# Second-layer tile stores and loads cut by groups of 32 partitions, spaced 7 units apart, with weights asked for 12 units ahead

## The chip, the cores and the metric

The kernel runs on one core of a Trainium2 chip. The time is the device time of one execution in microseconds; the median of three runs of the kernel before is 1767.69 us (1763.55, 1767.69 and 1768.19).

## The reference

```python
def _moe2_ref(x, U, V, w_ch1, w_ch2):
    xt = x.transpose(0, 2, 1)
    h = xt @ U @ V
    u = x + h.transpose(0, 2, 1)
    ch = np.maximum(u @ w_ch1, 0.0) @ w_ch2
    return (u + ch).astype(np.float32)

def reference(**kwargs):
    ...
    attn_out = _attn_ref(**attn_kwargs)
    B, H, S, D = attn_out.shape
    x = np.ascontiguousarray(attn_out.transpose(0, 2, 1, 3)).reshape(B, S, H * D)
    x = _moe_ref(x=x, **moe_kwargs)
    return _moe2_ref(x=x, **moe2_kwargs)
```

q, k and v are float32 of (8, 8, 576, 64). Attention works within chunks of 64 rows. Both layers that follow work on 8*576 = 4608 rows of 512 columns with weights of 512x2048 and 2048x512, which come in as float64. The first layer normalises its rows; the second adds a product of rank 32 along the sequence (U and V) before its two matrix products.

## The kernel before

The 4608 rows are 36 tiles of 128 rows. The first layer runs over 12 blocks of 3 tiles together with the attention, and leaves each finished tile in DRAM (`x1_d`, `store`, L698). It ends at about 965 us of the span. The second layer, which the change concerns, takes the rows in five passes `s` of 6, 8, 8, 8 and 6 tiles (`SB`). One pass is 2*7*8 = 112 units (`UNITS`): 7 products of 8 units for the first weight matrix and 7 products of 8 units for the second (a Strassen scheme with 7 block products). A unit is six matmuls of 128x128 against 512 columns (384 in the first and the last pass), and needs one weight tile of 128x512 float32, 256 KB.

**Weights.** `w_in(n)` (L973) issues the DMA of the weight tile of unit `n` from DRAM on the queue of SP (SyncE). 15 buffers are used in turn (`NWR`), so the tile of unit `n` can only be written when the matmuls of unit `n - 15` are over. At unit `n` the program issues `w_in(n + 14)` and then the side tasks of the unit.

**Side tasks.** A table (`side(u, fn, args)`) hangs further work on units. Each engine and each DMA queue takes its instructions strictly in program order; an instruction that waits holds up those behind it. For each of the tiles of the next pass:

- `x1_load` (L790) loads a tile of the first layer's result from DRAM into a window `xw` (two buffers) with four DMAs of 64 KB on SP's queue. Each of the four takes a block of 32 rows and spreads it over all 128 partitions, 512 bytes per run.
- `x1_turn` (L796) transposes the window into the operand `u` on DVE (VectorE), 11 units later.
- `low` (L808) adds the rank-32 product on top: matmuls into `pslow`, and an add on DVE (L823).

For each tile of the pass before:

- `y_turn` (L957) transposes the finished tile on DVE into `zt` (two buffers in turn).
- `y_store` (L965) stores `zt` to the output three units later, with four DMAs of 64 KB on SP's queue, again one for each block of 32 rows, from all 128 partitions. In the last pass half of them go on ScalarE's queue. A later `y_turn` into the same buffer waits until these DMAs have landed.

For each of the eight batches `z_load` (L647) loads the rank-32 sums with DMAs of 256 KB, each of which writes the same 32 rows to four groups of partitions (`to_broadcast([4, 32, DM])`), `z_sum` adds on GpSimd (L654) and `z_rep` copies on ScalarE (L661) and subtracts on DVE (L662). The first and the third pass hold two batches each, the second and the fourth one each, the last none.

On DVE the same queue also holds what PE (TensorE) needs: the evacuation of each product from PSUM (`g1_evac` L903, `g2_evac` L926) and the low parts of the operands (`h_lo` L882). So a `y_turn` or `x1_turn` that waits for a DMA holds up PE.

Of the kernel before, what the change touches and what calls it, by code (L numbers as in the profile page):

```python
# [18 lines left out]
def fused_kernel(ctx, tc, q, k, v, g_ln, w1_a, w2_a, U, V, w1_b, w2_b, out):  # L19
    nc = tc.nc  # L20
# [4 lines left out]
    P = 128  # L25
# [7 lines left out]
    SB = (6, 8, 8, 8, 6)  # L33
# [667 lines left out]

    O = (0, 1, 5, 6, 4, 2, 3)
    W_AT = ((0, 2, 6, 1, 3, 4, 5), (6, 0, 5, 1, 2, 3, 4))
    UNITS = 2 * 7 * NPR
    ORDER = []
    for a, b in ((0, 1), (2, 2), (3, 3), (4, 5), (6, 6)):
# [9 lines left out]
    def unit(n):  # L716
# [3 lines left out]
            return (s, which) + ORDER[r]  # L720
        return s, which, stages(s)[r // NPR], r % NPR
    NWR, NHR = 15, 8
    row0 = [sum(SB[:s]) * P for s in range(len(SB))]
    ncol = [SB[s] * P // 2 for s in range(len(SB))]
    made = {}
# [64 lines left out]
    def x1_load(s, t):  # L790
        i = row0[s] // P + t
        w = win[s, t] = t1.tile([P, 4, P], F32, tag=("w", "cvd")[i % 2], name="xw")
        for a in range(4):
            nc.sync.dma_start(out=w[:, a], in_=x1_d[i][32 * a:32 * a + 32].rearrange("j (g c) -> g j c", g=4))  # L794

    def x1_turn(s, t):  # L796
        w = win.pop((s, t)).rearrange("p a (i k) -> p a k i", k=KT)
# [167 lines left out]
    def y_store(s, t):  # L965
        z_tile(s, t)
        r = row0[s] + t * P
        z = zout.pop((s, t)).rearrange("p (a c) -> p a c", a=4)
        for a in range(4):
            eng = nc.scalar if s == len(SB) - 1 and a % 2 else nc.sync  # L970
            eng.dma_start(out=out[r:r + P].rearrange("(a j) (g c) -> a g j c", a=4, g=4)[a], in_=z[:, a])  # L971

    def w_in(n):  # L973
        if n < len(SB) * UNITS:
            s, which, i, p = unit(n)
            nc.sync.dma_start(out=f32(wring(n)), in_=w_d[which, p][W_AT[which][O[i]]])  # L976

    tasks = {}

    def side(u, fn, a):  # L980
        tasks.setdefault(u, []).append((fn, a))
# [4 lines left out]
    def all_units():  # L986
        late = []
        ps1, banks2 = {}, {}
        nb = 0
        for n in range(len(SB) * UNITS):  # L990
            s, which, i, p = unit(n)
            N = ncol[s]
            last = n >= len(SB) * UNITS - NPR
            chain = i in (1, 5)
            w_in(n + NWR - 1)
            for fn, a in tasks.pop(n, ()):
                fn(*a)
            if which == 0:
                if not chain:
                    tags = G1B if n < 20 else G1B + G2B[2:]  # L1000
                    ps1[p] = psp.tile([P, DM], F32, tag=tags[nb % len(tags)], name="ps1")
                    nb += 1
                ps = ps1[p]
                hi, lo = xring(s, i)
                w = w_of(n)
                c = 0
                for k_ in range(2):
                    for l, x in ((w(0, k_), hi), (w(0, k_), lo), (w(1, k_), hi)):
                        mm(ps[:, :N], l, x[:, k_], start=c == 0 and not chain, stop=c == 5, skip_group_check=i in (0, 1, 4, 5))
                        c += 1  # L1010
                late.append((g1_evac, (s, i, p, ps)))
            else:
                if p == 0 and not chain:
                    banks2[i] = [psp.tile([P, DM], F32, tag=G2B[2 * (i in (2, 4)) + t], name="ps2") for t in range(2)]
                ps2 = banks2[i - chain]
                for t in range(2):
                    todo = [p]
                    if last:
                        todo = range(NPR) if p == NPR - 1 else ()
                    for pp in todo:  # L1020
                        hi, lo = (a[:, :N] for a in hring((7 * s + stages(s).index(i)) * NPR + pp))
                        w = w_of(n - p + pp)
                        for c, (l, x) in enumerate(((w(0, t), hi), (w(0, t), lo), (w(1, t), hi))):
                            mm(ps2[t][:, :N], l, x, start=pp == 0 and c == 0 and not chain, stop=pp == NPR - 1 and c == 2, skip_group_check=i in (0, 1, 4, 5))
                    if p == NPR - 1 and not last:
                        g2_evac(s, i, (t,), ps2)
                    if last and todo:
                        g2_evac(s, i, (t,), ps2)
                        for tt_ in range(SB[s] // 2):
                            y_turn(s, tt_, (2 + t, 3 + t))  # L1030
                            if t:
                                y_store(s, tt_)
            while len(late) > (which == 0):
                fn, a = late.pop(0)
                fn(*a)
            yield n
# [3 lines left out]
    def l2_first(at):  # L1040
        e = NF * (NB - 1)
        for b in range(2):
            g = e - 1 + 6 * b
            at(g, z_load, b, 0)
            at(g, z_load, b, 1)
            for m in (1, 2, 3):
                at(g + 1 + m, z_sum, b, m)
                if m < 3:
                    at(g + 1 + m, z_load, b, m + 1)
            at(g + 5, z_rep, b)  # L1050
        for t in range(SB[0]):
            at(e + (0, 2, 2, 4, 5, 6, 7)[t], x1_load, 0, t)
            at(e + (2, 4, 5, 6, 7, 8, 9)[t], x1_turn, 0, t)
        for n, part in enumerate(low_parts(0)):
            at(e + 9 + n // 2, low, 0, part, ("m0", "m1"))
        for n in range(NWR - 1):
            at(e + 6 + n // 2, w_in, n)
        at(e + 12, x_hi, 0, 0)
        for k_ in range(2):
            at(e + 12, x_lo, 0, 0, k_, nc.vector)  # L1060
        x_parts(1, 0, 1, nc.vector)
        x_parts(4, 0, 2, nc.vector)
        done = 1
        for s in range(len(SB)):
            u0 = s * UNITS
            for i, u in ((3, 14), (4, 19), (5, 26), (6, 31)):
                x_parts(u0 + u, s, i, nc.gpsimd)
            for p in range(NPR):
                h_parts(u0 + 38 + p, s, 0, p)
                side(u0 + (43 if p < 4 else 47) + p % 4, h_t1, (s, p))  # L1070
                side(u0 + 51 + p, h_t, (s, 3, p))
                for i in range(1, 7):
                    h_parts(u0 + 56 + 8 * stages(s).index(i) + p - 7, s, i, p)
            if s:
                for t in range(2):
                    side(u0 + 1 + t, u_adds, (s - 1, t))
                for t in range(SB[s - 1]):
                    side(u0 + 8 + 5 * t, y_turn, (s - 1, t))
                    side(u0 + 11 + 5 * t, y_store, (s - 1, t))
            if s + 1 < len(SB):  # L1080
                turned = []
                for t in range(SB[s + 1]):
                    u = u0 + 14 + 6 * t
                    side(u, x1_load, (s + 1, t))
                    side(u + 11, x1_turn, (s + 1, t))
                    turned.append(u + 11)
                z0 = u0
                ready = 0
                for part in low_parts(s + 1):
                    b = part[2]  # L1090
                    if b > done:
                        for g in range(2):
                            side(z0, z_load, (b, g))
                        for g in (1, 2, 3):
                            z0 += 6
                            side(z0, z_sum, (b, g))
                            if g < 3:
                                side(z0, z_load, (b, g + 1))
                        z0 = ready = max(ready + 1, z0 + 2)
                        side(z0, z_rep, (b,))  # L1100
                        ready += 2
                        z0 += 1
                        done = b
                    ready = max(ready, turned[part[3]]) + 1
                    side(ready, low, (s + 1, part, G2B[:2] if ready < u0 + 54 else G1B))
                assert ready < u0 + 82, ready - u0
                x_parts(u0 + 96, s + 1, 0, nc.vector, 2)
                x_parts(u0 + 100, s + 1, 1, nc.vector, 2)
                x_parts(u0 + 105, s + 1, 2, nc.vector, 2)
            else:  # L1110
                for t in range(2):
                    side(u0 + 56 + 34 + 6 * t, u_adds, (s, t))
                n = SB[s] // 2
                for t in range(n):
                    side(u0 + 105 + t, y_turn, (s, n + t))
                    side(u0 + 107 + t, y_store, (s, n + t))
                    side(u0 + 108 + t, y_turn, (s, t, (0, 2)))


    with tc.manual_schedule():  # L1120
# [23 lines left out]
        for n in range(2, NB):  # L1144
            g = NF * (n - 1)
# [260 lines left out]
```

## Time and profile before

| what | value |
| --- | --- |
| median of three runs | 1767.69 us |
| the profiled execution | 1765.53 us |
| its span | 1763.7 us |
| PE busy (pipelined matmuls) | 1647.9 us, 93% |
| DVE, ScalarE, GpSimd busy | 1208.5, 599.4, 303.6 us |
| HBM read, written | 241.53 MB, 64.49 MB |

The span is one execution as the hardware profiler saw it; 1.8 us lie around it. PE's busy time counts overlapping matmuls, so that its share alone does not tell how close it is to its limit; the idle time and the time of one unit do. "DMA share" is the mean busy share of the core's 16 DMA engines.

### The profile page before, as it was taken

How to read it: one execution, taken by the hardware profiler on the slowest of the kernel's cores; microseconds unless marked ns; L12 is line 12 of the kernel's file. 1: busy time of each engine (PE TensorE's matmuls, PEld its weight loads, DVE VectorE, ACT ScalarE, POOL GpSimd, SP SyncE). 2: the span in 40 equal slices, each digit the busy share in tenths (PEclk: the TensorE clock that was granted, in tenths of full speed). 3: DMA queues.
4: the chain of work that ended last, by engine and by line, in shares of the span. 5: the costliest groups of instructions: out<-in, count | busy, mean ns of one | idle time of the engine just before them, and what ended most of it. 6: DMA issues, size and time to landing. Idle time of an engine off the chain costs nothing.

```text
span 1763.7 us, 27789 instructions
## 1 busy us (share of the span) xinstructions
PE 1647.9 (93%) x9902; PEld 1429.2 (81%) x9902; DVE 1208.5 (69%) x2226; ACT 599.4 (34%) x1098; POOL 303.6 (17%) x291
## 2 busy tenths in 40 slices
PE   6899999999999999999998889989995999899996
PEld 5788887888888888888887889868874888678995
DVE  7888645687777888788743368379535963785585
ACT  5554311223333332232321244334423343344342
POOL 1000001202111111111210240430133005301311
PEclk8899999999999999999999989999997999999998
DMA  6443333556557566575533678667765766677783
GB/s 168 114 138 108 84 83 87 148 146 167 166 143 200 161 170 177 151 213 157 180 112 117 199 222 282 195 218 247 194 191 168 226 193 192 204 231 198 244 275 114
DMA packets 380492, 307.90 MB, mean 175 GB/s; under 512 B 189505, under 2 KB 276545, under 8 KB 380354
## 3 DMA queue, kind: packets, MB, share of 16 engines
q1 hardware_dynamic: 317490, 247.12, 49.2%
q10 hardware_dynamic: 62864, 59.00, 10.5%
q8 instruction: 80, 1.31, 0.3%
q14 instruction: 58, 0.48, 0.1%
HBM read 241.53 MB, written 64.49 MB: 174 GB/s over the span
## 4 chain that ended last, share of the span: by engine, by line
PE 59%; DMA 7%; DVE 5%; SPq 2%; issue 1%; ACT 1%; POOL 0%; DVEq 0%; POOLq 0%; ACTq 0%
PE ps L66 32%; PE acc L66 13%; PE psh L66 12%; DMA zr<-zd 2%; DMA out<-zt 2%; DMA wr<-wd 1%; PE psm L66 1%; DMA xw<-x1d 1%; SPq L794 1%; DVE zt L963 1%; PE zps L66 1%; PE pslow L66 1%; SPq L971 0%; SPq L976 0%; POOL zr L654 0%
## 5 line engine op out<-in xcount | busy, mean ns | idle before, releaser
L66 PE MATMUL ps<-act,wr 128*128 128x512 f32 (+1 forms) x2100 | 460.3, 376 | 36.9 <-DVE h L918 9.8
L66 PEld LDWEIGHTS ps<-act,wr 128*128 128x128 f32 x2100 | 390.0, 192 | 96.2 <-issue 20.7
L66 PE MATMUL psh<-act,w0h 128*128 128x384 f32 x1536 | 398.4, 340 | 7.4 <-DVE act L679 2.8
L66 PE MATMUL acc<-w1h,act 128*128 128x512 f32 x1152 | 400.1, 401 | 1.6 <-DVE xbig L696 1.6
L66 PEld LDWEIGHTS psh<-act,w0h 128*128 128x128 f32 x1536 | 285.1, 190 | 26.7 <-DVE act L679 3.8
L66 PEld LDWEIGHTS acc<-w1h,act 128*128 128x128 f32 x1152 | 217.2, 189 | 58.7 <-issue 7.9
L66 PE MATMUL psh<-act,w0l 128*128 128x384 f32 x768 | 261.3, 340 | 0.9 <-DVE w0l L158 0.9
L679 DVE SCALAR_TENSOR_TENSOR act<-psh,act 128x384 fp32r<-128x384 f32 x192 | 106.8, 556 | 186.4 <-ACT act L678 185.9
L66 PE MATMUL acc<-w1l,act 128*128 128x512 f32 x576 | 228.1, 396 | 0.0
L678 ACT ACTIVATE act<-psh 128x384 fp32r<-128x384 f32 x192 | 94.0, 489 | 347.3 <-PE psh L66 284.2
L66 PEld LDWEIGHTS psh<-act,w0l 128*128 128x128 f32 x768 | 146.1, 190 | 1.2 <-DVE w0l L158 1.2
L66 PEld LDWEIGHTS acc<-w1l,act 128*128 128x128 f32 x576 | 108.7, 189 | 17.6
L908 ACT ACTIVATE h<-h 128x512 f32<-128x512 f32 (+1 forms) x80 | 45.8, 588 | 159.9 <-DVE h L918 120.0
L618 POOL TENSOR_TENSOR act<-wT,act 128x512 fp32r<-128x512 f32 x27 | 34.9, 1294 | 303.1 <-ACT act L617 303.1
L544 POOL TENSOR_SCALAR rs<-mv 128x1 f32<-128x1 f32 x36 | 10.9, 302 | 402.2 <-DVE mv L542 393.9
L914 DVE TENSOR_TENSOR h<-ps,h 128x512 f32<-128x512 f32 (+1 forms) x40 | 23.8, 628 | 62.9 <-PE ps L66 47.6
L654 POOL TENSOR_TENSOR zr<-zr 128x512 f32<-128x512 f32 x24 | 31.1, 1297 | 201.2 <-DMA zr<-zd 190.1
L197 ACT ACTIVATE raw<-raw 128x512 f32<-128x512 f32 x64 | 42.7, 675 | 53.1 <-DVE raw L228 13.4
L901 POOL TENSOR_TENSOR h<-h,h 128x512 f32<-128x512 f32 (+1 forms) x40 | 49.1, 1242 | 45.4 <-ACT h L908 25.0
L963 DVE STREAM_TRANSPOSE zt<-xbig 128x512 f32<-128x512 f32 (+1 forms) x16 | 15.3, 974 | 53.7 <-DMA out<-zt 36.0
L963 DVE STREAM_TRANSPOSE zt<-qk 128x256 f32<-128x256 f32 (+2 forms) x26 | 16.8, 690 | 45.0 <-DMA out<-zt 26.5
L564 POOL TENSOR_TENSOR xn<-xn,gbc 128x512 f32<-128x512 f32 x27 | 38.6, 1430 | 50.5 <-DVE xn L563 50.5
(218 smaller groups left out, 2623.5 us busy)
## 6 DMA issues: line engine op xcount, KB each, us to landing
wr<-wd SPq DMA_DIRECT2D x560, 256.0 KB
raw<-in_moe_w_ch SPq DMA_DIRECT2D x48, 512.0 KB
w<-sp ACTq DMA_DIRECT2D x54, 256.0 KB
wd<-wsp ACTq DMA_DIRECT2D x38, 256.0 KB
xw<-x1d SPq DMA_DIRECT2D x144, 64.0 KB
x1d<-xbig SPq DMA_DIRECT2D x34, 256.0 KB
v_pl<-in_v SPq DMA_DIRECT2D x132, 64.0 KB
out<-zt SPq DMA_DIRECT2D x132, 64.0 KB
```

What stands on the lines that cost most here:

```text
L66: nc.tensor.matmul(o, lhsT=l, rhs=r, start=start, stop=stop, **kw)
L197: nc.scalar.activation(out=w.bitcast(F32), in_=w.bitcast((F32, U32)[n]), func=AF.Copy, scale=2.0 ** (-112, -52)[n])
L564: nc.gpsimd.tensor_tensor(out=xn, in0=xn, in1=gbc, op=ALU.mult)
L618: nc.gpsimd.tensor_tensor(out=lo, in0=x, in1=f32(hi), op=ALU.subtract)
L654: nc.gpsimd.tensor_tensor(out=zr[:, 0], in0=zr[:, 0], in1=zr[:, 1], op=ALU.add)
L678: nc.scalar.activation(out=hi, in_=ps, func=AF.Relu)
L679: nc.vector.scalar_tensor_tensor(out=lo, in0=ps, scalar=0.0, in1=f32(hi), op0=ALU.max, op1=ALU.subtract)
L794: nc.sync.dma_start(out=w[:, a], in_=x1_d[i][32 * a:32 * a + 32].rearrange("j (g c) -> g j c", g=4))
L901: nc.gpsimd.tensor_tensor(out=b11, in0=b12, in1=b11, op=ALU.subtract)
L908: relu = lambda a: nc.scalar.activation(out=a, in_=a, func=AF.Relu)
L914: vt(out=c12, in0=ps, in1=c12, op=ALU.add)
L963: nc.vector.transpose(out=z[:, :, a:b], in_=u[:, a - k0:b - k0, o].rearrange("p k (a j) -> p a k j", j=32))
```

## The change

The four DMAs of `x1_load` and of `y_store` are cut in another way: each now moves one group of 32 partitions, with four runs of 512 bytes for each partition, where it moved one block of 32 rows to or from all 128 partitions. Bytes, number of DMAs and length of a run stay. `y_turn` of tile `t` stands at unit 8 + 7t of the pass (8 + 5t before) and `y_store` three units later as before; `x1_load` stands at unit 10 + 7t (14 + 6t) and `x1_turn` 11 units later as before. At unit `n` the program now issues `w_in(n + 12)`; there are still 15 buffers.

```diff
+    YT, XT = (8, 7, 3), (10, 7, 11)
...
     NWR, NHR = 15, 8
+    WL = NWR - 3
...
-        for a in range(4):
-            nc.sync.dma_start(out=w[:, a], in_=x1_d[i][32 * a:32 * a + 32].rearrange("j (g c) -> g j c", g=4))
+        for g in range(4):
+            nc.sync.dma_start(out=w[32 * g:32 * g + 32], in_=x1_d[i][:, g * P:(g + 1) * P].rearrange("(a j) c -> j a c", j=32))
...
-        for a in range(4):
-            eng = nc.scalar if s == len(SB) - 1 and a % 2 else nc.sync
-            eng.dma_start(out=out[r:r + P].rearrange("(a j) (g c) -> a g j c", a=4, g=4)[a], in_=z[:, a])
+        for g in range(4):
+            eng = nc.scalar if s == len(SB) - 1 and g % 2 else nc.sync
+            eng.dma_start(out=out[r:r + P, g * P:(g + 1) * P].rearrange("(a j) c -> j a c", j=32), in_=z[32 * g:32 * g + 32])
...
-            w_in(n + NWR - 1)
+            w_in(n + WL)
...
-                    side(u0 + 8 + 5 * t, y_turn, (s - 1, t))
-                    side(u0 + 11 + 5 * t, y_store, (s - 1, t))
+                    side(u0 + YT[0] + YT[1] * t, y_turn, (s - 1, t))
+                    side(u0 + YT[0] + YT[1] * t + YT[2], y_store, (s - 1, t))
...
-                    u = u0 + 14 + 6 * t
+                    u = u0 + XT[0] + XT[1] * t
                     side(u, x1_load, (s + 1, t))
-                    side(u + 11, x1_turn, (s + 1, t))
+                    side(u + XT[2], x1_turn, (s + 1, t))
```

SP's queue in the third pass, before: from the load of tile 112 to that of tile 113 (`xw` is the load's window, `zt` a store's source, `wr` a weight buffer; the last part of a row is the shape that the DMA writes).

```order
L794 DMA xw<-x1d_112 128x1x128 x4
L976 DMA wr_9357<-wd_5_131 128x512
L976 DMA wr_9450<-wd_6_132 128x512
L971 DMA out<-zt 4x32x128 x4
L976 DMA wr_9140<-wd_7_133 128x512
L976 DMA wr_9142<-wd_0_126 128x512
L976 DMA wr_9172<-wd_1_127 128x512
L976 DMA wr_9174<-wd_2_128 128x512
L794 DMA xw<-x1d_113 128x1x128 x4
```

The same stretch of SP's queue now:

```order
L796 DMA xw<-x1d_112 32x4x128 x4
L978 DMA wr_9244<-wd_7_133 128x512
L973 DMA out<-zt 32x4x128 x4
L978 DMA wr_9279<-wd_0_126 128x512
L650 DMA zr<-zd_147 128x1x512
L978 DMA wr_9281<-wd_1_127 128x512
L978 DMA wr_9317<-wd_2_128 128x512
L978 DMA wr_9319<-wd_3_129 128x512
L978 DMA wr_9446<-wd_4_130 128x512
L978 DMA wr_9458<-wd_5_131 128x512
L796 DMA xw<-x1d_113 32x4x128 x4
```

A store led by 4 becomes one led by 32, and so does the source of a load; seven weight tiles lie between two loads instead of six, and a store follows its load after one of them.

DVE's queue at the start of the third pass, before (L914 and L916 are evacuations that PE waits for, L963 is `y_turn`, L801 `x1_turn`):

```order
L963 STREAM_TRANSPOSE zt<-xbig 128x4x4x32
L914 TENSOR_TENSOR h_0_9604<-ps_12224,h_0_9604 128x512
L914 TENSOR_TENSOR h_0_9618<-ps_12235,h_0_9618 128x512
L801 STREAM_TRANSPOSE xbig<-xw 128x4x4x32
L916 TENSOR_TENSOR h_2_9674<-ps_12244,h_0_9472 128x512
L916 TENSOR_TENSOR h_2_9689<-ps_12254,h_0_9483 128x512
L916 TENSOR_TENSOR h_2_9702<-ps_12274,h_0_9503 128x512
L963 STREAM_TRANSPOSE zt<-xbig 128x4x3x32
```

The same stretch now:

```order
L965 STREAM_TRANSPOSE zt<-xbig 128x4x4x32
L916 TENSOR_TENSOR h_0_9597<-ps_12208,h_0_9597 128x512
L916 TENSOR_TENSOR h_0_9607<-ps_12219,h_0_9607 128x512
L916 TENSOR_TENSOR h_0_9621<-ps_12228,h_0_9621 128x512
L918 TENSOR_TENSOR h_2_9677<-ps_12242,h_0_9469 128x512
L918 TENSOR_TENSOR h_2_9692<-ps_12255,h_0_9481 128x512
L918 TENSOR_TENSOR h_2_9705<-ps_12266,h_0_9501 128x512
L803 STREAM_TRANSPOSE xbig<-xw 128x4x4x32
L918 TENSOR_TENSOR h_2_9719<-ps_12278,h_0_9512 128x512
L965 STREAM_TRANSPOSE zt<-xbig 128x4x4x32
```

Line numbers are two higher in the changed file. Between two `y_turn`s stand seven evacuations instead of five. The work itself is the same on every engine.

## Rows read from the trace of the kernel before

**Rows 1.** The page, parts 1 (busy time) and 4 (the chain, shares by line).
```profile
PE 1647.9 (93%) x9902; PEld 1429.2 (81%) x9902; DVE 1208.5 (69%) x2226; ACT 599.4 (34%) x1098; POOL 303.6 (17%) x291
...
PE ps L66 32%; PE acc L66 13%; PE psh L66 12%; DMA zr<-zd 2%; DMA out<-zt 2%; DMA wr<-wd 1%; PE psm L66 1%; DMA xw<-x1d 1%; SPq L794 1%; DVE zt L963 1%; PE zps L66 1%; PE pslow L66 1%; SPq L971 0%; SPq L976 0%; POOL zr L654 0%
```

**Rows 2.** Busy time in stretches: the five passes, then the tail.
```profile
core 0: us, PE busy (x) PEld busy (x) DVE busy (x) ACT busy (x) POOL busy (x), PEclk, DMA share, GB/s
967.00:1111.00 144.00, 130.94 (x707) 124.99 (x706) 92.10 (x170) 54.12 (x109) 28.84 (x26) 0.96 0.75 234
1111.00:1273.00 162.00, 156.16 (x683) 127.38 (x682) 110.16 (x173) 62.78 (x105) 35.52 (x30) 1.00 0.70 212
1273.00:1457.00 184.00, 162.84 (x694) 132.65 (x693) 111.63 (x177) 63.66 (x106) 41.55 (x33) 0.94 0.66 194
1457.00:1623.00 166.00, 157.81 (x687) 127.97 (x685) 108.00 (x172) 62.29 (x105) 38.33 (x29) 0.99 0.68 206
1623.00:1747.00 124.00, 119.90 (x673) 117.79 (x672) 81.98 (x150) 47.90 (x98) 35.51 (x32) 0.99 0.72 230
1747.00:1764.00 17.00, 0.00 (x0) 0.00 (x0) 4.84 (x13) 0.00 (x0) 0.00 (x0) 0.58 0.24 71
```

**Rows 3.** Timeline of ScalarE: first and 16th evacuation of the second and last pass.
```profile
1112.34 0.59 ACT L910 COPY h<-ps 128x512 f32<-128x512 f32 x1 [4.83 <-PE ps L66]
...
1132.73 0.60 ACT L912 ACTIVATE h<-ps 128x512 f32<-128x512 f32 x1 [0.76 <-PE ps L66]
...
1624.64 0.48 ACT L910 COPY h<-ps 128x384 f32<-128x384 f32 x1 [7.12 <-PE ps L66]
...
1640.24 0.49 ACT L912 ACTIVATE h<-ps 128x384 f32<-128x384 f32 x1 [0.55 <-PE ps L66]
```

**Rows 4.** Waits from 960 us on: total us, times, longest us.
```profile
DVE zt L963 <- DMA out<-zt: 62.5, 19, 8.1
...
DVE xbig L801 <- DMA xw<-x1d: 15.0, 4, 8.5
```

**Rows 5.** Timeline of DVE in the third pass: two `y_turn`s, idle before in brackets.
```profile
1332.08 0.85 DVE L963 STREAM_TRANSPOSE zt<-xbig 128x384 f32<-128x384 f32 x1 [8.07 <-DMA out<-zt]
...
1345.18 0.85 DVE L963 STREAM_TRANSPOSE zt<-xbig 128x384 f32<-128x384 f32 x1 [7.76 <-DMA out<-zt]
```

**Rows 6.** Timeline of SP's queue in the third pass: a held-up store and a free one.
```profile
1319.61 7.33 SPq L971 DMA_DIRECT2D out<-zt  x4
...
1360.41 2.43 SPq L971 DMA_DIRECT2D out<-zt  x4
```

**Rows 7.** Stretch of the tail with only stores: length, PE, clock, DMA share, GB/s.
```profile
1758.00:1759.00 1.00, 0.00 (x0) 0.50 0.29 87
```

**Rows 8.** SP's timeline and a stretch (columns as in 7): weight loads by 32 partitions.
```profile
57.25 1.74 SPq L130 DMA_DIRECT2D raw<-in_moe_w_ch  x4
...
59.00:60.00 1.00, 0.53 (x2) 0.50 0.91 268
```

**Rows 9.** Issues on SP's queue by line: duration ns min/median/max, first and last start.
```profile
L130 SPq DMA_DIRECT2D raw<-in_moe_w_ch x64: 311/428/1624, 5.0 to 176.6; - x64
...
L976 SPq DMA_DIRECT2D wr<-wd x560: 314/325/2145, 922.7 to 1731.1; - x187
...
L971 SPq DMA_DIRECT2D out<-zt x132: 536/567/2496, 1126.8 to 1755.8; - x132
```

**Rows 10.** Timeline of GpSimd in the first pass: a `z_sum` and what it waited for.
```profile
1013.93 1.27 POOL L654 TENSOR_TENSOR zr<-zr 128x512 f32<-128x512 f32 x1 [14.38 <-DMA zr<-zd]
```

**Rows 11.** Busy time in a stretch at the end of the first layer.
```profile
940.00:960.00 20.00, 16.59 (x79) 14.97 (x80) 7.06 (x12) 3.77 (x7) 1.85 (x2) 0.83 0.29 109
```

**Rows 12.** Timelines of SP's queue and of DVE in the tail.
```profile
1740.97 15.32 SPq L971 DMA_DIRECT2D out<-zt  x12
...
1746.93 0.63 DVE L963 STREAM_TRANSPOSE zt<-qk 128x256 f32<-128x256 f32 x1 [4.60 <-DMA out<-zt]
```

**Rows 13.** Busy time in a stretch in the middle of the second pass.
```profile
1202.00:1212.00 10.00, 10.00 (x45) 7.88 (x44) 10.00 (x19) 5.40 (x9) 0.00 (x0) 1.00 0.85 298
```

More of the change, by code (lines that the diff above doesn't have):

```diff
@@ L1055, in l2_first @@
             at(e + 9 + n // 2, low, 0, part, ("m0", "m1"))
-        for n in range(NWR - 1):
+        for n in range(WL):
             at(e + 6 + n // 2, w_in, n)
@@ L1082, in l2_first @@
                 for t in range(SB[s + 1]):
-                    u = u0 + 14 + 6 * t
+                    u = u0 + XT[0] + XT[1] * t
                     side(u, x1_load, (s + 1, t))
-                    side(u + 11, x1_turn, (s + 1, t))
-                    turned.append(u + 11)
+                    side(u + XT[2], x1_turn, (s + 1, t))
+                    turned.append(u + XT[2])
                 z0 = u0
```

## The prediction

> **What bounds the kernel now.** I read the page first, then stretches of the second layer, then what ended the waits there. PE is busy for 93% of the span, and its matmuls make up most of the chain; of DMAs the chain names the z loads, the stores of `zt` and the window loads with 1 to 2% each [rows 1]. So a gain can only come from stretches in which PE stands still or runs at the low clock, and these have to be sized.
>
> For that I need the length of a unit at full rate. In the second pass 15 units take 1132.73 - 1112.34 = 20.39 us, so 1.36 us; in the last pass 1640.24 - 1624.64 = 15.6 us, so 1.04 us [rows 3]. A pass of 112 units should take 152.2 or 116.5 us. The stretches of [rows 2] are cut one unit before each pass's first evacuation. From the 512-column passes I take off 2 us for the `pslow` matmuls (an estimate), and from the first pass 8 us for first-layer matmuls still among its units, `pslow` and `zps`. What is lost:
>
> - first pass: 144 - 116.5 - 8 = 19.5 us
> - second: 162 - 154.2 = 7.8 us
> - third: 184 - 154.2 = 29.8 us, at a mean clock of 0.94
> - fourth: 166 - 154.2 = 11.8 us
> - last: 124 - 116.5 = 7.5 us
> - tail, with PE idle: 17 us
>
> Together 93 us. Inside the passes DVE waits 62.5 us for output stores to land, in 19 places, and 15 us for window loads [rows 4]; in the third pass two `y_turn`s stand 8.07 and 7.76 us each [rows 5], with PE's evacuations queued behind them. Stores are late at their issue too: four took 7.33 us on SP's queue, where four others took 2.43 us [rows 6], and the weights queue behind.
>
> **Why the transfers are slow.** In the tail, with nothing but stores under way, the DMA share is 0.29 and 87 GB/s move [rows 7], though 24 DMAs are queued. That is little more than 4 of 16 engines, and the shape of a store is led by 4. I read it so: a store, a window load (its source is led by 4) and a z load (4 copies in front) each use four engines only, the same four, at 87/4 = 21.8 GB/s each. Against that, four weight loads by groups of 32 partitions, issued in 1.74 us, move 268 GB/s at a share of 0.91 [rows 8]. The new DMAs are led by 32 as well.
>
> [...]
>
> **A bound per pass.** I count what the four engines must move in the first 60 units of a pass, where the side tasks lie. A weight tile puts 16 KB on each, a tile's load or store 64 KB before and 16 KB now, a z load 64 KB in both. At 21.8 GB/s:
>
> - third pass (8 loads, 8 stores, 8 z loads): 0.98 + 0.52 + 0.52 + 0.52 = 2.55 MB, 117 us, where 60 units last 82 us: 35 us over. Now 0.98 + 0.13 + 0.13 + 0.52 = 1.77 MB, 81 us: just level.
> - second (4 z loads): 23 us over before, now 69 of 82 us.
> - fourth (6 loads, 4 z loads): 17 us over, now below 69 us.
> - last (stores alone): 69 of 62 us, 7 over; now 51.
> - first (8 loads, 8 z loads): 93 of 62 us, 31 over; now 75, still 13 over.
>
> The order of these overruns (35, 31, 23, 17, 7) is near that of the losses (29.8, 19.5, 7.8, 11.8, 7.5); 15 weight buffers absorb a part.
>
> **The change part by part.**
>
> - Third pass: 24 of 29.8 us go. The z loads stay on four engines, which come out just level, so some 5 us of waits remain. Bounds 12 and 29.
> - Second pass 7 of 7.8 us (bounds 3 and 7.8), fourth 10 of 11.8 us (6 and 11.8): the overrun is gone.
> - Last pass: 5 of 7.5 us (1 and 7).
> - First pass: 13 of 31 us of overrun stays, so 19.5 x 13/31 = 8 us of loss; 11 us go. What holds up the rest is a z sum, which stands 14.38 us before its DMA lands [rows 10]. Bounds 0 and 16.
> - End of the first layer, where window and z loads for the first pass share the four engines: PE is busy 16.59 of 20 us in one stretch, at a clock of 0.83 and a DMA share of 0.29 [rows 11]. The window loads get out of the z loads' way: 3 us (0 and 6).
> - Tail: `y_turn` waits 4.60 us for a store, and SP needs 15.32 us to issue 12 stores, as the engines are full [rows 12]. Without the wait DVE ends some 2 to 4 us earlier; the last 12 DMAs of 64 KB, 0.79 MB, need 9.0 us at 87 GB/s and 2.9 us at 268 GB/s, but at least 6 x 0.57 = 3.4 us to issue on each of two queues [rows 7 to 9]. 8 us of the 17 go (5 and 10).
> - Spacing: 11 units (15 us) lie between a store and the next `y_turn` into its buffer, where there were 7 (9.5 us). It adds nothing of its own to the sum, as the transfers themselves get short; it keeps SP's queue below full. Per tile that is 4 x 0.57 for the store, as much for the load and 7 x 0.4 for weights (0.33 and the wait for a free buffer), 7.4 us in the 9.5 us of 7 units [rows 9]; before it was about 6.8 us in 5 to 6 units, which last 6.8 to 8.2 us.
> - Issue price of the new shape: the nearest rows are 0.43 us for the weight loads led by 32 and 0.57 us for the old stores [rows 9]. I take the latter, and no change. Ends: 0.31 and 1.62 us (the extremes of the first).
> - Weights 12 units ahead: a tile still goes into a buffer freed 15 units before, so it can be written no later than now as long as SP is not held up. What moves is SP's other work: it waits for the matmuls of unit n - 3, not n - 1, and so comes two units (2.7 us) earlier. Cost nothing; if SP is held up, 12 units (16 us, or 12.5 us at 384 columns) are the cover.
> - Turns at later units: one or two `y_turn`s per pass move into units 50 to 57, where DVE is full (10.00 of 10 us, PE still 10.00 [rows 13]). At about 1 us each, with low parts due several units ahead: nothing, at most 2 us in each of three passes.
>
> Sum: 24 + 7 + 10 + 5 + 11 + 3 + 8 = 68 us. The profiled execution took 1765.5 us, so 1697.5 us; the median of the runs is 2.2 us above it, so **1700 us**. All low bounds give 27 us, all high ones 88 us.
>
> **The rivals.**
>
> 1. *The z loads set the pace.* They keep four engines, their sums wait on GpSimd, and ScalarE and DVE wait behind them. For it: 14.38 us [rows 10]; the passes with two batches lose most. Against it: the longest stands on DVE are for stores [rows 5]. Then the first pass gains only 2, the third 8 and the first layer nothing: 2 + 7 + 8 + 10 + 5 + 8 = 40 us, 1728 us.
> 2. *The cut by partitions brings no speed.* Only the spacing helps, and the four engines stay over their limit: some 10 us, 1757 us. [...] The 268 GB/s of [rows 8] speak against it.
> 3. *Slower: issuing on SP becomes the bound.* Eight tile DMAs and seven weight tiles must fit into the 9.5 us of 7 units. Beyond (9.5 - 2.8)/8 = 0.84 us per tile DMA every tile costs PE time. At 1.2 us it is 8 x 1.2 + 2.8 - 9.5 = 2.9 us for each of 30 tiles, 87 us, against 68 us gained: 1787 us. It outweighs the gain from 1.12 us on. For it: single issues took up to 1.62 us [rows 9]; against: the medians, and long issues before lie where the engines are full.
> 4. *DVE becomes the bound* in units 38 to 60, as the later turns meet the low parts: 3 x 4 us of the gain, 1712 us.
>
> **How the numbers follow.** Forecast (1681 to 1716 us) 0.66, rival 1 (1716 to 1745) 0.20, rival 4 0.03, rival 2 0.05, rival 3 0.04; 0.02 for a change that cancels out. About 0.3%, 5 us, is what a measurement of this kernel can tell from no change. So faster 0.94, same 0.02, slower 0.04. The range from 1680 to 1732 us holds the forecast, rival 4 and most of rival 1, some 0.82.
>
> **What the profile will show.** If I am right: DVE's wait for `out<-zt` falls from 62.5 us to under 10 us; the third pass takes under 162 us and the second and fourth under 157 us; the DMA share in the tail's last microseconds is well over 0.29, and the tail takes about 9 us; an issue of `out<-zt` stays near 0.57 us. Rival 1 shows in GpSimd's waits for z loads unchanged and a third pass above 170 us; rival 2 in a tail still at 87 GB/s; rival 3 in an issue median above 0.84 us; rival 4 in PE waiting for `hr` low parts of DVE. I would be wrong altogether if PE began to wait for weight tiles.

## The result, and the profile after

The changed kernel takes 1695.38 us, the median of four runs (1692.39 to 1698.08); the kernel before, measured beside it, took 1767.65. The ratio is 0.9596, with a 95% interval of 0.9574 to 0.9617. The forecast was 1700 us, in a range of 1680 to 1732. The profiled execution of after took 1696.09 us, its span 1694.2, against 1765.53 and 1763.7 before.

On the page, part 1, PE is busy for 96% instead of 93% [rows 1], with the same number of instructions on every engine:

```profile
PE 1633.8 (96%) x9902; PEld 1423.1 (84%) x9902; DVE 1210.2 (71%) x2226; ACT 599.7 (35%) x1098; POOL 307.0 (18%) x291
```

The busy time in stretches of after, cut like [rows 2]: the five passes, the tail, and two single microseconds of the tail.

```profile
core 0: us, PE busy (x) PEld busy (x) DVE busy (x) ACT busy (x) POOL busy (x), PEclk, DMA share, GB/s
968.00:1099.00 131.00, 127.19 (x713) 123.06 (x711) 92.01 (x172) 54.34 (x109) 28.31 (x25) 0.99 0.84 257
1099.00:1254.00 155.00, 154.66 (x679) 127.11 (x680) 109.98 (x172) 62.88 (x105) 35.63 (x29) 1.00 0.76 221
1254.00:1412.00 158.00, 156.44 (x694) 128.65 (x693) 114.06 (x177) 63.82 (x106) 45.41 (x32) 1.00 0.79 227
1412.00:1567.00 155.00, 155.00 (x689) 127.91 (x689) 108.55 (x173) 62.47 (x105) 38.57 (x29) 1.00 0.76 221
1567.00:1685.00 118.00, 117.61 (x675) 116.36 (x673) 83.86 (x152) 48.25 (x98) 35.18 (x32) 1.00 0.79 244
1685.00:1694.00 9.00, 0.29 (x2) 0.00 (x0) 3.84 (x11) 0.00 (x0) 0.00 (x0) 0.65 0.43 117
1690.00:1691.00 1.00, 0.00 (x0) 0.00 (x0) 0.00 (x0) 0.00 (x0) 0.00 (x0) 0.50 0.95 258
1691.00:1692.00 1.00, 0.00 (x0) 0.00 (x0) 0.00 (x0) 0.00 (x0) 0.00 (x0) 0.50 0.92 252
```

The gain lies in all five passes and in the tail. PE idles 0.3 of 155 us in the second pass and not at all in the fourth, and the clock of the third is 1.00 where it was 0.94. The tail is 9 us long instead of 17, and its end moves 258 GB/s at a DMA share of 0.95 instead of 87 at 0.29 [rows 7].

DVE's waits for DMAs from 960 us on (total us, times, longest) fell from 62.5 and 15.0 [rows 4] and 12.7 us to 3.1 and 3.0. The 12.7 us are two `y_turn`s whose wait the profile puts down to a window load; a `y_turn` neither reads nor writes a window, so these are probably waits for stores too. The wait of 3.0 us ends at 1683.9 us, just before PE's last matmul. One line of before, then two of after:

```profile
DVE zt L963 <- DMA xw<-x1d: 12.7, 2, 7.4
...
DVE xbig L803 <- DMA xw<-x1d: 3.1, 1, 3.1
DVE zt L965 <- DMA out<-zt: 3.0, 1, 3.0
```

PE gained by it: from 960 us on it waited 37.9 us in all for DVE before, and 0.3 in after, where what is left is 5.1 us of waits for weight tiles (5.7 before). The longest line of before and of after:

```profile
PE pslow L66 <- DVE xbig L823: 10.1, 2, 7.5
...
PE ps L66 <- DMA wr<-wd: 5.1, 3, 2.7
```

SP's queue in after's third pass, and its stores in the tail. The store is at 2.33 us, near the free one of [rows 6], but a window load still took 5.66; the tail's twelve stores take 11.65 us instead of 15.32 [rows 12].

```profile
1304.39 5.66 SPq L796 DMA_DIRECT2D xw<-x1d  x4
...
1311.06 2.33 SPq L973 DMA_DIRECT2D out<-zt  x4
...
1679.60 11.65 SPq L973 DMA_DIRECT2D out<-zt  x12
```

The issues in after (duration in ns, min/median/max): a store's DMA takes 337 ns at the median where it took 567 [rows 9]. The z loads, which the change leaves alone, stay at 525.

```profile
L973 SPq DMA_DIRECT2D out<-zt x132: 315/337/1686, 1117.8 to 1690.8; - x132
...
L796 SPq DMA_DIRECT2D xw<-x1d x144: 302/422/1491, 884.2 to 1475.9; - x144
...
L650 SPq DMA_DIRECT2D zr<-zd x32: 508/525/623, 879.6 to 1433.3; - x32
```

One place got no better: at the end of the first layer PE is still busy for only 15.94 of 20 us, at a clock of 0.83 [rows 11].

```profile
940.00:960.00 20.00, 15.94 (x72) 13.98 (x71) 6.88 (x12) 3.27 (x6) 2.56 (x2) 0.83 0.43 135
```

### The profile page after: what moved, and what is told of

Same layout as the page of the kernel before. It is cut to its first block, busy times and chain, and to the rows that moved or that the text cites. A ratio compares the mean times of both kernels' runs of the same rounds, so it can differ in the third digit from the quotient of the medians.

```text
span 1694.2 us, 27810 instructions
## 1 busy us (share of the span) xinstructions
PE 1633.8 (96%) x9902; PEld 1423.1 (84%) x9902; DVE 1210.2 (71%) x2226; ACT 599.7 (35%) x1098; POOL 307.0 (18%) x291
## 4 chain that ended last, share of the span: by engine, by line
PE 62%; DMA 7%; DVE 4%; issue 1%; ACT 0%; SPq 0%; POOL 0%; ACTq 0%; DVEq 0%; POOLq 0%
PE ps L66 37%; PE acc L66 12%; PE psh L66 11%; DMA wr<-wd 3%; DMA zr<-zd 2%; PE psm L66 1%; DMA raw<-in_moe_w_ch 1%; DMA wd<-wsp 1%; PE zps L66 1%; PE pslow L66 1%; DMA wd<-wsq 0%; DVE zt L965 0%; DVE raw L228 0%; DMA out<-zt 0%; DVE act L679 0%
## 5 line engine op out<-in xcount | busy, mean ns | idle before, releaser
L66 PE MATMUL ps<-act,wr 128*128 128x512 f32 (+1 forms) x2100 | 445.7, 369 | 5.4 <-DMA wr<-wd 5.1
L66 PEld LDWEIGHTS ps<-act,wr 128*128 128x128 f32 x2100 | 382.8, 188 | 58.3 <-DMA wr<-wd 5.2
L910 ACT ACTIVATE h<-h 128x512 f32<-128x512 f32 (+1 forms) x80 | 46.3, 588 | 102.8 <-DVE h L920 83.7
L916 DVE TENSOR_TENSOR h<-ps,h 128x512 f32<-128x512 f32 (+1 forms) x40 | 24.7, 632 | 69.7 <-PE ps L66 68.5
L66 PE MATMUL ps<-hr0h,wr 128*128 128x512 f32 (+1 forms) x140 | 46.7, 373 | 0.3 <-issue 0.2
L66 PE MATMUL ps<-hr1h,wr 128*128 128x512 f32 (+1 forms) x140 | 46.0, 368 | 0.0
```

Of the source, the lines that this page charges most:

```text
L66: nc.tensor.matmul(o, lhsT=l, rhs=r, start=start, stop=stop, **kw)
L910: relu = lambda a: nc.scalar.activation(out=a, in_=a, func=AF.Relu)
L916: vt(out=c12, in0=ps, in1=c12, op=ALU.add)
```

## The experiments

Twelve kernels were run beside the kernel before. "Start" is the first evacuation of the first pass on ScalarE, a pass is the time between the first evacuations of two passes, and the last column goes from the last pass's first evacuation to the end of the span; these come from the profiled executions, in us. The start is not steady: the kernel before, the stores' cut alone and the spacing alone share all code up to the first pass, and start it at 966.8, 962.1 and 974.1. So two single starts are not compared, only groups of kernels that lie apart.

| kernel | median | ratio, interval | start | 1 | 2 | 3 | 4 | 5 + tail |
|---|---|---|---|---|---|---|---|---|
| before | 1767.65 | | 966.8 | 145.5 | 161.7 | 184.0 | 166.6 | 139.1 |
| after | 1695.38 | 0.960 (0.957 to 0.962) | 968.9 | 131.8 | 155.3 | 157.9 | 155.1 | 125.3 |
| cut alone | 1710.54 | 0.969 (0.967 to 0.971) | 964.0 | 136.0 | 154.9 | 170.7 | 158.3 | 125.7 |
| stores' cut alone | 1724.98 | 0.977 (0.974 to 0.980) | 962.1 | 144.9 | 154.9 | 172.3 | 158.5 | 125.6 |
| loads' cut alone | 1744.75 | 0.989 (0.986 to 0.991) | 964.4 | 136.6 | 158.1 | 179.6 | 162.9 | 137.9 |
| spacing and 12 units | 1727.99 | 0.980 (0.977 to 0.983) | 968.1 | 137.6 | 158.0 | 171.2 | 156.2 | 133.2 |
| spacing alone | 1734.59 | 0.982 (0.978 to 0.985) | 974.1 | 141.0 | 157.6 | 172.5 | 160.1 | 133.4 |
| 12 units alone | 1754.07 | 0.993 (0.991 to 0.996) | 967.6 | 142.4 | 159.4 | 180.9 | 164.6 | 136.8 |
| cut and 12 units | 1704.10 | 0.966 (0.963 to 0.970) | 964.7 | 133.8 | 154.9 | 166.1 | 155.9 | 125.8 |
| cut and spacing | 1699.19 | 0.962 (0.959 to 0.964) | 964.7 | 135.1 | 155.3 | 160.1 | 155.6 | 125.4 |
| z loads cut alone | 1726.89 | 0.978 (0.976 to 0.981) | 956.5 | 134.2 | 156.0 | 172.9 | 163.3 | 138.6 |
| after + z loads cut | 1677.34 | 0.950 (0.947 to 0.952) | 953.7 | 127.2 | 155.3 | 155.6 | 155.1 | 125.3 |
| the same + buffer | 1676.71 | 0.950 (0.947 to 0.953) | 958.9 | 127.6 | 155.3 | 156.0 | 155.1 | 123.4 |
| cut by 16 | 1788.36 | 1.012 (1.009 to 1.015) | 972.0 | 150.8 | 167.2 | 188.3 | 172.2 | 136.8 |

The theory, read from the tail's DMA share of 0.29 (4.6 of 16 engines) [rows 7] and the shapes, was that the transfers' leading count of 4 confines them to four DMA engines; the rivals were the spacing, and SP's time for issuing.

**The cut alone**: the two shapes of the change in the kernel before.

```diff
-        for a in range(4):
-            nc.sync.dma_start(out=w[:, a], in_=x1_d[i][32 * a:32 * a + 32].rearrange("j (g c) -> g j c", g=4))
+        for g in range(4):
+            nc.sync.dma_start(out=w[32 * g:32 * g + 32], in_=x1_d[i][:, g * P:(g + 1) * P].rearrange("(a j) c -> j a c", j=32))
...
-            eng.dma_start(out=out[r:r + P].rearrange("(a j) (g c) -> a g j c", a=4, g=4)[a], in_=z[:, a])
+            eng.dma_start(out=out[r:r + P, g * P:(g + 1) * P].rearrange("(a j) c -> j a c", j=32), in_=z[32 * g:32 * g + 32])
```

> Only the cut of the loads and stores is changed; spacing and the 14 units stay. If the four engines are what is short, nearly the whole gain comes from the cut alone: 1696 to 1706 us. If the spacing carries half of the gain (rival), 1725 to 1735 us. If the cut brings no speed, 1760 us or more.

1710.54 us: 56 us of the gain with the queues' order as before, though less than was expected. DVE's wait for stores is halved, not gone, and the third pass stays at 170.7 us. Pass by pass the cut alone takes off 9.5, 6.8, 13.3 and 8.3 us, and 13.4 in the last pass with the tail.

```profile
DVE zt L963 <- DMA out<-zt: 29.5, 11, 8.2
```

**Spacing and 12 units, without the cut**: the change with the old two shapes.

> The changed kernel with the old cut put back: the spacing and the 12 units alone. The four engines have the same bytes to move in nearly the same units, so by my theory a gain of about 10 us, 1750 to 1762 us, and DVE still waits 40 us or more for stores. By the rival (the spacing carries the gain) 1725 us or less.

1727.99 us, a miss of 22 us and more. With stores still led by 4, DVE waits 13.0 us for them instead of 62.5 (waits from 960 us on):

```profile
DVE xbig L803 <- DMA xw<-x1d: 16.6, 6, 5.4
...
DVE zt L965 <- DMA out<-zt: 13.0, 7, 4.1
```

So most of the waits go when the transfers are only spread out, or the weights asked for later. The next two runs part these.

**Spacing alone**: the kernel of the last run with the weights 14 units ahead again.

```diff
-    WL = NWR - 3
+    WL = NWR - 1
```

> Old cut and 14 units, only the spacing of 7. If spacing and the 12 units add up, 1766 - (38 - 12) = 1740 us (1733 to 1747); if they do the same thing twice, 1724 to 1732 us.

1734.59 us, as expected if the two add up: the spacing is worth 31 us by itself.

**12 units alone**: one number of the kernel before, at its two places.

```diff
-            w_in(n + NWR - 1)
+            w_in(n + NWR - 3)
...
-        for n in range(NWR - 1):
+        for n in range(NWR - 3):
```

> Only the 12 units instead of 14. By my theory it moves loads and stores on SP by two units and costs and gives nothing: 1760 to 1770 us. A rival (SP standing behind weight tiles makes the stores late) gives 1745 us or less; another (weights come late) 1775 us or more.

1754.07 us, 12 us faster and a second miss. The parts' gains overlap: 56 + 31 + 12 = 99 us, where all three give 72.

**Cut and spacing**: after with `WL = NWR - 1`.

> The changed kernel with 14 units put back. By my theory the 12 units do nothing: 1693 to 1700 us. If they carry something, 1702 us or more.

**Cut and 12 units**: after with the old table.

```diff
-    YT, XT = (8, 7, 3), (10, 7, 11)
+    YT, XT = (8, 5, 3), (14, 6, 11)
```

> The changed kernel with the old spacing: the cut and the 12 units. Between the 1710.5 us of the cut alone and the 1695 us of the whole. If the 12 units only spare waits that the cut spares too, 1705 to 1711 us, and the spacing is worth 10 us or more; if they add up, 1696 to 1702 us.

1699.19 and 1704.10 us. On top of the cut and the 12 units the spacing is still worth 8.7 us, nearly all of it in the third pass (166.1 to 157.9). On top of the cut and the spacing the 12 units give 3.8 us, with intervals that overlap: not told apart from nothing. The 1704.10 us lie between the two ranges that were given. The cut and the spacing together give 67 us, where 56 and 31 would make 87, and the spacing and the 12 units give 38, where 31 and 12 would make 43: the overlap lies mostly between the cut and the spacing.

**Stores' cut alone and loads' cut alone**: one of the two shapes each.

> Only the stores get the new cut. Counting bytes on four engines: third pass 17 us over instead of 35, second 5 instead of 23, fourth and last none, first unchanged; with 8 us of the tail a gain of about 44 us, 1715 to 1732 us. If what counts is the wait of the turn for its store and not the engines, the whole gain inside the passes comes from the stores: 1705 us or less.

> Only the window loads get the new cut. Counting bytes: third pass 15 us gained, second 6, fourth 9, first 11, last none, the first layer's end 3, the tail none: about 44 us, 1715 to 1732 us, and DVE waits less for stores though these keep the old cut. If the turn's wait for its own store is what counts, a gain of under 20 us: 1748 us or more.

The first pass loads tiles but stores none. There the stores' cut does nothing (144.9 us), and the loads' cut takes 9 us off; in the last pass, which only stores, it is the other way round, and the whole gain of the tail is the stores'. That is as the count of bytes per pass would have it. But the loads' cut gained 21 us in all, where as much as for the stores was expected (about 44 us), a third miss: with the stores on their old shape DVE still waits for them 45.6 us, in 19 places, as often as before:

```profile
DVE zt L963 <- DMA out<-zt: 45.6, 19, 5.5
```

**The z loads cut alone**: stores, loads and table as before. Four DMAs of 64 KB, each led by 32, write the copies, where one of 256 KB was led by the count of 4.

```diff
-        nc.sync.dma_start(out=zr_t[b][:, g % 2 if g < 2 else 1], in_=z_d[b][32 * g:32 * g + 32, :].unsqueeze(0).to_broadcast([4, 32, DM]))
+        for m in range(4):
+            nc.sync.dma_start(out=zr_t[b][32 * m:32 * m + 32, g % 2 if g < 2 else 1], in_=z_d[b][32 * g:32 * g + 32, :])
```

> The kernel before with each z load cut into four DMAs by groups of 32 partitions; loads and stores keep the old cut. If z loads use the same four engines, taking them away relieves the first and third pass by about 11 and 15 us, the others by a few: 1725 to 1745 us. If z loads do not share the engines (rival), 1760 us or more.

1726.89 us, as expected. This run bears most on the theory: not one store or window load is changed, and SP issues 96 DMAs more, yet DVE's wait for stores falls from 62.5 to 43.1 us (all waits of `y_turn`s, whatever DMA the profile names, from 75.2 to 55.7). The last pass, which has no z loads, gains nothing by it (138.6 us with the tail, beside 139.1).

```profile
DVE zt L964 <- DMA out<-zt: 43.1, 14, 5.4
```

The three kinds of transfer thus share something that is short, and it is not SP's time for issuing.

**After with the z loads cut**: the edit of the last run in after.

> The changed kernel, with the z loads cut by groups of 32 partitions too. The first pass still loses by z loads and late weights: 8 us of it go, and 2 us at the first layer's end and in the third pass each: 1681 to 1690 us. If z loads do not matter any more, 1693 us or more; if the extra issues on SP make weights late, slower than 1697 us.

1677.34 us, faster than both kernels and better than expected. Stretches of it: the first and the third pass, and the last 20 us of the first layer at the place that answers to after's 940 to 960.

```profile
core 0: us, PE busy (x) PEld busy (x) DVE busy (x) ACT busy (x) POOL busy (x), PEclk, DMA share, GB/s
953.00:1079.00 126.00, 124.58 (x710) 121.61 (x709) 93.17 (x171) 54.69 (x109) 28.34 (x25) 1.00 0.86 266
...
1235.00:1390.00 155.00, 155.00 (x691) 128.17 (x690) 113.57 (x176) 63.90 (x106) 42.82 (x32) 1.00 0.78 230
...
925.00:945.00 20.00, 20.00 (x108) 18.32 (x107) 7.60 (x15) 3.78 (x7) 2.58 (x2) 1.00 0.52 171
```

PE is busy for the whole of the 20 us of which after lost 4, at a clock of 1.00 instead of 0.83. The three kernels with this cut start the first pass at 953.7 to 958.9 us and the eleven others at 962.1 to 974.1; in the stretch from 29 to 9 us before that start PE is busy for 19.2 to 20.0 us in the three, at a clock of 1.00, and for 14.5 to 16.5 in the eleven, at 0.74 to 0.91. How much of the 15 us between the starts of these two profiles is spread is not known. The third pass is at the length of the second and the fourth. What stood there is the subtraction at the end of a z batch, in DVE's timeline of after and then of this kernel (idle time before it in brackets):

```profile
943.09 1.06 DVE L662 TENSOR_TENSOR zs<-zr,zs 64x512 fp32r<-64x512 f32 x1 [5.77 <-ACT zs L661]
```

```profile
929.53 1.07 DVE L663 TENSOR_TENSOR zs<-zr,zs 64x512 fp32r<-64x512 f32 x1 [0.44 <-ACT zs L662]
```

**The same with a buffer of its own for the last pass's last tile**, to take away the wait of 3.0 us at its end.

```diff
-... else ("xn", "gbc")[t % 2], name="zt")
+... else "cvd" if s == len(SB) - 1 and t == SB[s] - 1 else ("xn", "gbc")[t % 2], name="zt")
```

> The kernel with all three cut by groups of 32 (1677 us), and the last output tile in a buffer of its own, so that no turn waits for a store in the tail (3.0 us). If that wait stands on the path to the end, 1672 to 1675 us; if PE's last matmuls set the end, 1676 to 1679 us.

1676.71 us, not told apart from 1677.34, and in the range given for PE's last matmuls setting the end. The wait is gone and last pass and tail are 1.9 us shorter in the profile, but that profile's first pass began 5 us later.

**Cut by 16**: the tile DMAs in eight parts of 32 KB, led by 16 partitions, in the kernel before.

```diff
+        for m in range(8):
+            g, q_ = divmod(m, 2)
+            nc.sync.dma_start(out=w[16 * m:16 * m + 16], in_=x1_d[i][:, g * P:(g + 1) * P].rearrange("(a j) c -> j a c", j=32)[16 * q_:16 * q_ + 16])
```

(the same for the store)

> The kernel before with loads and stores cut by groups of 16 partitions, eight DMAs of 32 KB each for a tile, old spacing and 14 units. [...] If the engines count, still far faster than before, 1708 to 1730 us. If the gain of the cut came from shorter issuing on SP (rival), no faster than before, 1766 us or more.

1788.36 us: slower than before, a miss, and the outcome that was named for the rival by which the cut gains through shorter issuing on SP. The median of an issue was 0.42 us for half the bytes:

```profile
L973 SPq DMA_DIRECT2D out<-zt x264: 315/417/2078, 1136.8 to 1784.0; - x132
```

Eight stores or loads then hold SP's queue for 4 to 7 us, here at the start of the second pass:

```profile
1136.80 6.89 SPq L973 DMA_DIRECT2D out<-zt  x8
...
1145.83 6.66 SPq L795 DMA_DIRECT2D xw<-x1d  x8
...
1153.52 3.68 SPq L973 DMA_DIRECT2D out<-zt  x8
...
1159.40 4.25 SPq L795 DMA_DIRECT2D xw<-x1d  x8
```

The first two of these in the kernel before, with four DMAs each:

```profile
1126.81 5.10 SPq L971 DMA_DIRECT2D out<-zt  x4
...
1135.37 4.29 SPq L794 DMA_DIRECT2D xw<-x1d  x4
```

By the medians a store, a load and some six weight tiles come to 16 x 0.42 + 6 x 0.33 = 8.7 us for the 6.8 to 8.2 us of 5 to 6 units, which would fill SP's queue. The trace does not bear this out: in the 31 us from 1134 on, issues take 21.8 us, and the first two groups hold pauses of 2.3 and 2.8 us, of which no run gives the reason. The first pause:

```profile
1136.80 0.85 SPq L973 DMA_DIRECT2D out<-zt  x2
...
1139.94 0.32 SPq L973 DMA_DIRECT2D out<-zt  x1
```

In the second pass all issues on SP together take 90.1 us, as in the kernel before (90.3). PE's waits for weight tiles grew from 5.7 to 13.6 us. What made the kernel slower stays open.

The same sums bear on the rival. They are 89.4 us with the spacing alone and 90.5 with the z loads cut alone, so these two gain without less issuing. With the cut alone the sum falls to 66.8 us. How much of its 56 us comes from there, and how much from stores and loads that land sooner, was not told apart inside the passes; in the tail issuing can be ruled out (see the next section).

How many engines a DMA led by 16 uses, and whether as many as one led by 32, stays open too. The tail moves 135 GB/s at a share of 0.53, and two queues that issue 32 KB in 0.42 us each cannot fill more than 156. But stretches of 0.2 us reach a share of 0.68, which is 11 of 16 engines, so these DMAs are not held to four:

```profile
1780.80:1781.00 0.20, 0.00 (x0) 0.00 (x0) 0.00 (x0) 0.00 (x0) 0.00 (x0) 0.50 0.68 187
...
1782.00:1783.00 1.00, 0.00 (x0) 0.00 (x0) 0.00 (x0) 0.00 (x0) 0.00 (x0) 0.50 0.53 135
```

## Why the prediction was right, and where it was not

Before and after by the table above, with the tail apart (PE ended at 1746.7 before and at 1685.3 in after):

| term | predicted gain | measured |
|---|---|---|
| end of the first layer | 3 | -2.1 |
| first pass | 11 | 13.7 |
| second pass | 7 | 6.4 |
| third pass | 24 | 26.2 |
| fourth pass | 10 | 11.5 |
| last pass | 5 | 5.6 |
| tail | 8 | 8.1 |
| sum | 68 | 69.4 |

The terms of the passes and of the tail held one by one, because each was taken from what a pass loses against its own full rate: an upper bound that the change nearly reached. That they were reached in the way that was given is true only in part. The third pass, priced at 24 us for the cut, gains 13.3 by the cut alone, and the rest came with the spacing, which was priced at nothing. To that extent the fit of the sum is luck.

The signs that the prediction named are there too: a wait for stores of 3.0 us (under 10), a third pass of 157.9 (under 162), a second and fourth of 155.3 and 155.1 (under 157), a tail of 9 us at a share of 0.95. PE does not wait more for weight tiles than before. GpSimd's waits for z loads, which rival 1 would have left unchanged, fell from 139.2 to 102.8 us (from 960 us on).

Three things bear out the reading that the old shapes share few engines, about four of 16: the tail's share of 0.29 (4.6 of 16) and its 87 GB/s with nothing else under way, and with the last store issued by 1757.15 us, so that issuing cannot be what held them; the passes in which the stores' cut or the loads' cut alone gains (last pass and tail 125.6 and 137.9 us for 139.1, first pass 144.9 and 136.6 for 145.5); and the z loads' cut, which shortens the stores' waits from 62.5 to 43.1 us without touching them. The end of the issues in the tail before, on ScalarE's queue, the later of the two, and a stretch behind it (columns as in [rows 7]):

```profile
1740.98 16.17 ACTq L971 DMA_DIRECT2D out<-zt  x12
...
1760.00:1761.00 1.00, 0.00 (x0) 0.50 0.29 86
```

No trace here tells one engine from another. The prices in the prediction's count per pass, 16 KB of a weight tile or of a tile in the new shape on each engine (256 KB over 16) and 64 KB of the old shapes and the z loads (over four), are thus the author's estimate, and no run shows them; what the runs show is the share with stores alone under way, 0.29 before and 0.95 in after (15.2 of 16). That the old shapes use the same four is not shown either; the stores' waits under the z loads' cut show that the two share something. Of rival 2's sign, a tail still at 87 GB/s, nothing is left: it ends at 258 GB/s, and the cut alone, without the spacing, gives a ratio of 0.969.

Five steps were wrong; none took the sum out of the range:

- **Spacing "adds nothing of its own to the sum"**, and rival 2's price of some 10 us for it. It is worth 31 us alone and 8.7 us on top of the cut and the 12 units. The count over the first 60 units saw how many bytes there are and not how thick they lie, nor how long a buffer can wait for them. By the prediction's own prices, where loads and stores overlap, a unit put 16.4 KB of weights, 65.5/5 of stores and 65.5/6 of loads on each of the four engines, 40.4 KB, and at 21.8 GB/s 1.36 us take 29.6; at every 7 units it is 35.1 KB. Half of the excess goes, and a store has 15 us to land where it had 9.5. This is worked out, not measured; that the waits for stores fall to 13.0 us with the old shape is measured. The sum came out right because the spacing's gain is mostly the same idle time that the cut takes (20 of its 31 us, by the run with both).
- **Weights 12 units ahead "cost nothing"**: true, but they gain 12 us alone. The reason given for no loss, that SP's other work comes two units earlier, is a reason for a gain where the stores are late; that this is the cause was not tested. Beside the cut and the spacing no gain can be told from nothing.
- **Issue price "no change" at 0.57 us.** It fell to 0.34 for stores and 0.42 for loads; the other row, 0.43 of the weight loads led by 32, was the nearer. With the cut alone stores took 0.42 as well. Nor were full engines shown to be why SP needed 15.32 us for the tail's twelve stores: their issues took 536 to 676 ns each, and between them, by SP's waits in the trace of before, the queue stood 7.0 us for `y_turn`s.
- **End of the first layer, 3 us.** It was put down to window loads that get out of the way; the -2.1 lies within the spread of the starts, so no gain can be read. The z loads themselves hold this stretch, as their cut showed (PE busy for 19.2 to 20.0 of 20 us with it, 14.5 to 16.5 without).
- **Second pass, 23 us over.** It stores the six tiles of the first pass, not eight, so that the same count gives 2.16 MB, 99 us, 17 us over, as for the fourth. The order of the overruns fits the losses a little better so; the term of 7 us was taken from the loss and stands. The first pass's stretch, too, begins at its first evacuation and not a unit before it, so its loss was some 1 us more.

Rival 1 (the z loads set the pace, 1728 us) was wrong in its size, but its mechanism is real: it is what is left after the change, 18 us. In after DVE stands 5.77 us before a z batch's subtraction, and the first and third pass are 4.6 and 2.3 us longer than with the z loads cut. Rival 3 (SP's issuing becomes the bound) did not happen: the price fell. The cut by 16, which doubles the issues, lost 22 us, but with SP issuing no longer than before, so it does not show this rival. Of rival 4 nothing is seen: the second and fourth passes, which it would hold up, are at full rate, and PE waits for no low part in after (1.5 us before, from 960 us on).

## What to carry to other kernels

Compare the rate of a stretch in which one kind of transfer runs alone with the best rate in the trace; where it is a small part of it, as the 87 GB/s here [rows 7], where other stretches moved 268 and 298 [rows 8, 13], look at the leading count of both sides of the DMA (the stores' tail ended at 258 GB/s when led by 32 instead of 4), and at every other transfer with a small one: here the z loads' cut alone took DVE's wait for stores from 62.5 to 43.1 us. Size the gain by what each stage loses against its own full rate, and test order and shape apart: here spreading the same slow transfers gave more than half of what making them fast gave. Cut no finer than needed: the same bytes in twice the DMAs, led by 16, turned a gain of 56 us into a loss of 22, for a reason that stays open.

## What was not expected of the hardware

The time that an issue takes on SP's queue was longest for DMAs led by 4, and the bytes hardly mattered. Led by 4 it was 567 ns for a store of 64 KB, 530 for a window load of 64 KB and 525 for a z load of 256 KB (medians, kernel before), and never under 507. Led by 16 a store of 32 KB took 417, led by 32 a window load took 422 and a z load of 64 KB 413, and the weight tiles of 256 KB, led by 128, took 320 in after. Between 16 and 128 no order is shown, as one shape differs as much between two kernels: the store led by 32 has a median of 337 in after and of 422 with the cut alone. The window load in the kernel before, and the store with the cut alone:

```profile
L794 SPq DMA_DIRECT2D xw<-x1d x144: 507/530/3197, 879.9 to 1537.6; - x144
...
L971 SPq DMA_DIRECT2D out<-zt x132: 315/422/1786, 1114.0 to 1706.3; - x132
```

Cutting a z load in four thus costs SP 1.65 us instead of 0.53, and gains by it.
